# A PE-saturated attention kernel: the five score steps of a head pair in another order, issued ahead of the softmax parts, and the first pair's steps on other slots

## The chip, the cores and the metric

The kernel runs on one core of one Trainium2 chip. The metric is the device time of one execution in microseconds (us); three runs of the kernel before gave 687.08, 687.08 and 687.57, so the median is 687.08. TensorE is called PE below and its weight loads PEld, VectorE is DVE, ScalarE is ACT, GpSimd is POOL, SyncE (which issues most DMAs) is SP.

## The reference

An input x of 2048 tokens by 448 features is normalised, and two branches are added to it: attention with 16 heads of 28 features, in four segments of 512 tokens with a compressive memory, and a gated FFN of width 1792.

```python
logits = jnp.einsum("bhqd,bhkd->bhqk", qs, ks) * scale + mask   # per segment, 512 x 512
p = _softmax(logits, axis=-1)
a_dot = jnp.einsum("bhqk,bhkd->bhqd", p, vs)
a_mem = num / den                                 # recall from the memory of earlier segments
o = g * a_mem + (1.0 - g) * a_dot
...
h = _sigmoid(g) * u                               # FFN
return x + _A_ref(xn, ...) + _B_ref(xn, ...)
```

The mask keeps only a triangle of each 512 by 512 block: in this reference's orientation, with keys in four blocks of 128 rows, block kb meets 512 - 128 kb query columns: 512, 384, 256 and 128.

## The kernel before, in words

**Stages.** A front part (to about 160 us) normalises x, turns it, and computes keys, queries, values and the memory. Then the FFN runs on PE, and the attention of all segments is cut into small steps that are dropped between the FFN's matmul groups. Last comes the output projection (`project`, lines 749 to 783), which begins when the FFN's own groups are out.

**FFN.** `gated` (line 166) loops over pairs of 128 wide slices and over the four token blocks. For each slice it runs two groups of 11 matmuls of 512 columns (`pgu`, line 247), and the down projection of the block before in groups of 6 matmuls of 448 columns (`pd`, line 173).

**Attention.** A `Pair` is two heads of one segment; a `Unit` is two pairs (four heads); there are 32 pairs and 16 units. `Pair.scores` (lines 603 to 637) has five steps, n = 0 to 4. Each step runs one or two matmuls `st` (line 612) into one PSUM bank of 512 columns (tag "s", two banks), ACT copies the bank into the pair's SBUF tile `w` (line 616 or 619), POOL writes the mask into the diagonal blocks (line 627), and after some steps DVE takes maxima with a transposing reduction (`mx`, line 629 for 1024 columns, line 633 for 512). Before the change the steps are: head 0 block 512; head 0 blocks 384+128 and the reduction of head 0; head 1 block 512; head 1 blocks 384+128 and the reduction of head 1; both heads' blocks of 256 and their short reduction.

`Pair.weights` (lines 639 to 668) has five parts: the maxima are joined by small DVE and POOL operations (lines 643 to 653), DVE spreads them (`mb`, line 656), and three times DVE subtracts (line 666) and ACT takes the exponential (line 667). `Unit.finish` (lines 681 to 695) multiplies the weights of four heads with the values (`pa`, line 687, 32 matmuls in the profile), divides (lines 690 to 693) and adds the result into DRAM (`od`, line 694).

**What sets the order.** `attention` (line 700) walks for each unit over the 14 entries of `SLOT` (line 39): 0 or 1 means one score step of the unit's first or second pair, 2 means `finish` of the unit before, `None` means no step. In each slot it first gives out one part of the weights waiting in `behind`, then the second half of a `finish`, then the score step. When a pair's last score step is out, its five weight parts are appended to `behind` (line 724), and the SP queue gets the six DMAs (line 595) that load the keys and queries of the pair two further on; for the last unit these are instead the eight DMAs (line 747) of `load_sums(0)` and `load_sums(1)`, which fetch the finished attention rows for the projection. After a `finish` the unit's values are loaded (`vv`, line 679). The loop at lines 789 to 798 gives out 234 slots evenly over the FFN's and the projection's steps.

On PE and SP the program's order is kept (`MANUAL`, line 55). On ACT, DVE and POOL a planner places the instructions when the kernel is built; there the order of the program only decides which goes first when several are ready in its plan. The buffers are: `w` three, `mx` two, `mb`, `up`, `top` one, keys and queries (`qk2`) two, PSUM tag "s" two banks.

Of the kernel before, what the change touches and what calls it, by code (L numbers as in the profile page):

```python
# [16 lines left out]
P = 128  # L17
# [5 lines left out]
L = 512  # L23
# [12 lines left out]
LEAD, TAIL = 15, 53  # L36


SLOT = (0, 0, 0, None, 0, 0, None, 2, 1, 1, 1, None, 1, 1)

PARTS = 5

# [1 line left out]
HW = 1280  # L44
# [17 lines left out]
def kernel(  # L62
# [11 lines left out]
    V, A, G, T = nc.vector, nc.scalar, nc.gpsimd, nc.tensor  # L74
# [40 lines left out]
    def bank(name, tag):  # L115
        return ps.tile([P, L], F32, name=name, tag=tag, bufs=banks[tag])
# [159 lines left out]
    with tc.tile_pool(name="front", bufs=2) as sb, tc.manual_schedule(engines=FRONT):  # L276
# [227 lines left out]
        for b in range(NB):  # L504
# [24 lines left out]
            for k, c in enumerate((3, 4, 5, 6, 0, 1, 2) if last else range(7)):  # L529
# [34 lines left out]
                n = k - 1 if b == 0 else k + 1  # L564
# [18 lines left out]
    class Pair:  # L583
# [19 lines left out]
        def scores(self):  # L603

            self.w = sb.tile([P, 2 * HW], F32, name="w", bufs=3)
            w3 = self.w.rearrange("p (h n) -> p h n", h=2)
            mx = sb.tile([P, 80], F32, name="mx", bufs=2)
            for n in range(5):
                st = bank("st", "s")
                for h, kb in (((n // 2, 0),), ((n // 2, 1), (n // 2, 3)))[n % 2] if n < 4 else ((0, 2), (1, 2)):  # L610
                    at = KB[kb] % L + (256 * h if kb == 2 else 0)
                    T.matmul(st[:, at:at + L - kb * P], self.qk[:KS, 1, h, kb * P:(kb + 1) * P],  # L612
                             self.qk[:KS, 0, h, kb * P:], start=True, stop=True)
                if n < 4:
                    w = self.w[:, HW * (n // 2) + L * (n % 2):][:, :L]
                    A.activation(w, st, AF.Copy)  # L616
                else:
                    w = w3[:, :, 2 * L:]
                    A.activation(w, st.rearrange("p (h n) -> p h n", h=2), AF.Copy)

                if n % 2 == 0 and n < 4:
                    d = w[:, :P]
                    pattern = [[1, P]]
                else:
                    d = w.rearrange("p (a n) -> p a n", n=P)[:, 0:4:3, :] if n < 4 else w[:, :, :P]
                    pattern = [[0, 2], [1, P]]
                G.affine_select(d, d, pattern=pattern, base=0, channel_multiplier=-1, compare_op=ALU.is_ge, fill=MASK)  # L627
                if n in (1, 3):
                    V.tensor_reduce(mx[:, 16 * (n - 1):16 * (n + 1)],  # L629
                                    w3[:, n // 2, :2 * L].rearrange("p (b n) -> p b n", n=32),  # L630
                                    axis=mybir.AxisListType.X, op=ALU.max, apply_transpose=True)
                if n == 4:
                    V.tensor_reduce(mx[:, 64:80].rearrange("p (h b) -> p h b", h=2),
                                    w.rearrange("p h (b n) -> p h b n", n=32),
                                    axis=mybir.AxisListType.X, op=ALU.max, apply_transpose=True)
                yield
            yield from self.weights(mx)
# [60 lines left out]
    units = [Unit(u, pairs[2 * u:2 * u + 2]) for u in range(NB * NG)]  # L698

    def attention():  # L700
        for n in range(2):
            pairs[n].load()
        units[0].load_values()
        yield
        run, behind, fin = {}, [], None
        for u in range(len(units) + 1):
            for n in range(2):
                run[n] = pairs[2 * u + n].scores() if u < len(units) else iter(())
            for k, which in enumerate(SLOT):
                if u == len(units):  # L710

                    if k > 9:
                        break
                    which = ((None,) * 8 + (2, None))[k]
                if behind:
                    next(behind.pop(0))
                if fin:
                    next(fin)
                    fin = None
                if which is not None and which < 2 and u < len(units):  # L720
                    next(run[which])
                    n = 2 * u + which + 2
                    if which not in SLOT[k + 1:]:
                        behind += [run[which]] * PARTS
                        if n < len(pairs):
                            pairs[n].load()
                        else:
                            load_sums(n - len(pairs))
                if which == 2 and u > 0:
                    fin = units[u - 1].finish()  # L730
                    next(fin)
                    if u < len(units):
                        units[u].load_values()
                yield
# [3 lines left out]
    def load_sums(b):  # L738

        if b < 2:  # L740
            sums[b] = sb.tile([P, HG, L], F32, name="sums", tag="qk2", bufs=2)
        else:
            sums[b] = sums[b - 2]
        o3 = od[b].rearrange("(h c) n -> h c n", c=32)
        for m in range(8):
            a, c = m % 2, 4 * min(m, 6)
            nc.sync.dma_start(sums[b][64 * a:64 * a + 64, m // 2, :], o3[:, c:c + 4, :])  # L747
# [36 lines left out]

    N_OUT = 1 + NB * NT * 3 + 12
    steps = attention()
    n_att = len(units) * len(SLOT) + 10
    done = 0
    with tc.manual_schedule(engines=MANUAL):
        next(steps)  # L790
        k = sum(FILLS) + 6
# [46 lines left out]
```

## Time and profile before

| what | value |
|---|---|
| median of three runs | 687.08 us |
| the profiled execution | 687.17 us |
| its span, first to last instruction | 685.5 us |
| granted TensorE clock | 1.0 of full speed |
| busy: PE, DVE, PEld | 99%, 83%, 83% of the span |
| busy: ACT, POOL | 50%, 21% of the span |
| DMA | 84.37 MB, mean 123 GB/s |

The busy time of an engine is the time covered by its instructions. The end of a matmul in the profile is modelled, and matmuls overlap, so the distance from one start to the next says more than the duration of one. "Idle before" tells how long an engine stood still ahead of a group, and the name behind the arrow is what released it. A timeline row has the start in us, the length in us, the engine, the line, the operation, what it writes and reads, and how many instructions are merged into the row. Groups of one line give how often, and the minimum, median and maximum of one in ns.

### The profile page before, as it was taken

How to read it: one execution, taken by the hardware profiler on the slowest of the kernel's cores; microseconds unless marked ns; L12 is line 12 of the kernel's file. 1: busy time of each engine (PE TensorE's matmuls, PEld its weight loads, DVE VectorE, ACT ScalarE, POOL GpSimd, SP SyncE). 2: the span in 40 equal slices, each digit the busy share in tenths (PEclk: the TensorE clock that was granted, in tenths of full speed). 3: DMA queues.
4: the chain of work that ended last, by engine and by line, in shares of the span. 5: the costliest groups of instructions: out<-in, count | busy, mean ns of one | idle time of the engine just before them, and what ended most of it. 6: DMA issues, size and time to landing. Idle time of an engine off the chain costs nothing.

```text
span 685.5 us, 10454 instructions
## 1 busy us (share of the span) xinstructions
PE 680.3 (99%) x3594; PEld 566.1 (83%) x3594; DVE 567.1 (83%) x995; ACT 341.6 (50%) x563; POOL 146.6 (21%) x349
## 2 busy tenths in 40 slices
PE   8999999999999999999999999999999999999998
PEld 7898878778878787887878778787887878778897
DVE  6765695767789998988998889988998899889863
ACT  4837555343554455544556446455643465446220
POOL 3500010101223232222232222222322313212000
PEclk9999999999999999999999999999999999999999
DMA  7446556697232333243324243324342423423352
GB/s 268 178 153 232 205 205 245 244 336 182 71 95 76 95 88 86 57 126 80 90 59 107 62 126 72 99 57 117 81 99 73 97 56 83 94 77 96 92 156 107
DMA packets 45940, 84.37 MB, mean 123 GB/s; under 512 B 6336, under 2 KB 20544, under 8 KB 45376
## 3 DMA queue, kind: packets, MB, share of 16 engines
q1 hardware_dynamic: 42736, 76.26, 36.2%
q0 software_dynamic: 3008, 7.34, 5.1%
q8 instruction: 28, 0.46, 0.3%
q14 instruction: 24, 0.20, 0.1%
q10 hardware_dynamic: 144, 0.11, 0.0%
HBM read 51.05 MB, written 32.64 MB: 122 GB/s over the span
## 4 chain that ended last, share of the span: by engine, by line
PE 96%; DMA 1%; SPq 1%; DVE 1%; issue 0%; ACT 0%; DVEq 0%; ACTq 0%
PE pgu L247 41%; PE pd L173 20%; PE pp L355 10%; PE st L612 6%; PE po L771 5%; PE pa L687 5%; PE pv L335 5%; PE pmm L383 2%; PE n L401 2%; DMA acc<-in_x 1%; SPq L747 1%; PE pt L95 1%; PE pk L375 1%; DMA vv<-vd 0%; DVE stats L294 0%
## 5 line engine op out<-in xcount | busy, mean ns | idle before, releaser
L247 PE MATMUL pgu<-xs,wgu 128*128 128x512 f32 x1232 | 303.6, 393 | 0.0
L247 PEld LDWEIGHTS pgu<-xs,wgu 128*128 128x128 f32 x1232 | 228.2, 188 | 46.9 <-issue 2.4
L173 PE MATMUL pd<-wdn,hh 128*128 128x448 f32 x672 | 155.9, 367 | 0.0
L173 PEld LDWEIGHTS pd<-wdn,hh 128*128 128x128 f32 x672 | 122.4, 188 | 12.0 <-issue 0.8
L627 POOL TENSOR_SCALAR_AFFINE_SELECT w<-w 128x256 f32<-128x256 f32 (+1 forms) x160 | 79.7, 501 | 242.0 <-ACT w L616 193.1
L667 ACT ACTIVATE w<-w 128x1024 f32<-128x1024 f32 (+1 forms) x96 | 87.3, 915 | 87.3 <-DVE w L666 86.8
L666 DVE TENSOR_TENSOR w<-w,mb 128x1024 f32<-128x1024 f32 (+1 forms) x96 | 98.7, 1036 | 0.2
L616 ACT ACTIVATE w<-st 128x512 f32<-128x512 f32 x128 | 74.6, 590 | 43.5 <-PE st L612 43.2
L629 DVE TRANSPOSE_TENSOR_REDUCE mx<-w 128x32 f32<-128x1024 f32 x64 | 78.8, 1231 | 14.9 <-POOL w L627 14.9
L355 PE MATMUL pp<-xs,wqk 128*128 128x512 f32 x308 | 77.7, 401 | 0.0
L174 DVE TENSOR_TENSOR acc<-pd,acc 128x448 f32<-128x448 f32 x112 | 67.2, 600 | 1.1 <-PE pd L173 1.1
L355 PEld LDWEIGHTS pp<-xs,wqk 128*128 128x128 f32 x308 | 56.8, 188 | 13.4 <-issue 2.4
L612 PE MATMUL st<-qk 84*128 84x128 f32 (+3 forms) x256 | 62.2, 312 | 0.1
L258 ACT ACTIVATE hh<-sg 128x512 fp32r<-128x512 f32 x56 | 35.2, 628 | 52.5 <-DVE sg L256 41.9
L612 PEld LDWEIGHTS st<-qk 84*128 84x128 f32 x256 | 47.6, 189 | 7.4 <-ACT w L616 0.6
L255 ACT ACTIVATE sg<-pgu 128x512 f32<-128x512 f32 x56 | 33.1, 591 | 37.5 <-PE pgu L247 37.4
L656 DVE STREAM_TRANSPOSE mb<-top 128x1024 f32<-128x1024 f32 x32 | 39.7, 1242 | 12.5 <-POOL top L653 12.2
L362 DVE TENSOR_TENSOR qk<-pp,qk 128x512 fp32r<-128x512 f32 x28 | 19.3, 688 | 29.8 <-ACT e L360 23.7
L259 DVE SCALAR_TENSOR_TENSOR hh<-sg,hh 128x512 fp32r<-128x512 f32 x56 | 38.9, 694 | 2.8 <-ACT hh L258 2.4
L335 PE MATMUL pv<-wv,xs 128*128 128x448 f32 x176 | 39.7, 376 | 0.2
L256 DVE SCALAR_TENSOR_TENSOR sg<-sg,pgu 128x512 f32<-128x512 f32 x56 | 37.4, 667 | 1.8 <-PE pgu L247 1.6
L687 PE MATMUL pa<-w,vv 128*32 128x128 f32 (+3 forms) x512 | 37.9, 436 | 0.0
(100 smaller groups left out, 640.7 us busy)
## 6 DMA issues: line engine op xcount, KB each, us to landing
qk<-qd SPq DMA_DIRECT2D x192, 112.0 KB
qd<-qk SPq DMA_DIRECT2D x28, 512.0 KB
raw<-in_w_ffn SPq DMA_DIRECT2D x14, 512.0 KB
vd<-vst SPq DMA_DIRECT2D x4, 1024.0 KB
vv<-vd SPq DMA_DIRECT2D x16, 256.0 KB
od<-w POOLq DMA_DIRECT2D x16, 256.0 KB, 4.0
sums<-od SPq DMA_DIRECT2D x32, 128.0 KB
out<-acc SPq DMA_DIRECT2D x15, 224.0 KB
```

The source lines that it names most:

```text
L173: T.matmul(pd[:, :D], l, r, start=n == 0, stop=n == len(mms) - 1)
L174: V.tensor_add(acc[b][:, t, :], pd[:, :D], acc[b][:, t, :])
L247: T.matmul(dst, wgu[f][:, w, side * P:(side + 1) * P], xs[b][:, a, :], start=n == 0, stop=n == len(TERMS) - 1)
L335: T.matmul(pv[:, :D], xs[b][:, a, t * P:(t + 1) * P], wv[w], start=n == 0, stop=n == len(TERMS) - 1)
L355: T.matmul(pp, wqk[c][:, w, :], xs[b][:, a, :], start=n == 0, stop=n == len(TERMS) - 1)
L612: T.matmul(st[:, at:at + L - kb * P], self.qk[:KS, 1, h, kb * P:(kb + 1) * P], self.qk[:KS, 0, h, kb * P:], start=True, stop=True)
L616: A.activation(w, st, AF.Copy)
L627: G.affine_select(d, d, pattern=pattern, base=0, channel_multiplier=-1, compare_op=ALU.is_ge, fill=MASK)
L629: V.tensor_reduce(mx[:, 16 * (n - 1):16 * (n + 1)], w3[:, n // 2, :2 * L].rearrange("p (b n) -> p b n", n=32), axis=mybir.AxisListType.X, ...
L666: V.tensor_sub(w, w, m)
L667: A.activation(w, w, AF.Exp, scale=SCALE)
L687: T.matmul(pa[32 * j:32 * j + 32, kb * P:], self.vv[:, kb, 32 * j:32 * j + 32], self.pairs[j // 2].block(j % 2, kb), start=kb == 0, stop=k ...
```

## The change

Three things are changed, and nothing is computed otherwise.

The score steps of a pair come in another order: head 0 block 512; head 1 block 512; both heads' blocks of 256, with their short reduction; head 0 blocks 384+128, with head 0's reduction; head 1 blocks 384+128, with head 1's reduction.

A score step is cut in two by a `yield`: matmuls, ACT copy and POOL mask are given out first, then the weights part that is due in the slot and the second half of a `finish`, then the DVE reduction.

The first pair's steps sit on slots 1, 2, 4, 5 and 7 where they sat on 0, 1, 2, 4 and 5. The second pair's stay on 8, 9, 10, 12 and 13, and `finish` stays on 7, where the first pair's last step is now ahead of it.

```diff
-SLOT = (0, 0, 0, None, 0, 0, None, 2, 1, 1, 1, None, 1, 1)
+SLOT = ((), (0,), (0,), (), (0,), (0,), (), (0, 2), (1,), (1,), (1,), (), (1,), (1,))
...
-                for h, kb in (((n // 2, 0),), ((n // 2, 1), (n // 2, 3)))[n % 2] if n < 4 else ((0, 2), (1, 2)):
+                h = n % 2 if n < 2 else n - 3
+                for h, kb in (((h, 0),), ((0, 2), (1, 2)), ((h, 1), (h, 3)))[(0, 0, 1, 2, 2)[n]]:
...
                 G.affine_select(d, d, pattern=pattern, base=0, channel_multiplier=-1, compare_op=ALU.is_ge, fill=MASK)
-                if n in (1, 3):
-                    V.tensor_reduce(mx[:, 16 * (n - 1):16 * (n + 1)],
-                                    w3[:, n // 2, :2 * L].rearrange("p (b n) -> p b n", n=32),
+                yield
+                if n > 2:
+                    V.tensor_reduce(mx[:, 32 * h:32 * h + 32],
+                                    w3[:, h, :2 * L].rearrange("p (b n) -> p b n", n=32),
                                     axis=mybir.AxisListType.X, op=ALU.max, apply_transpose=True)
-                if n == 4:
+                if n == 2:
...
+                score = [which for which in now if which < 2]
+                part = behind.pop(0) if behind else None
+                for which in score:
+                    next(run[which])
+                if part:
+                    next(part)
                 if fin:
                     next(fin)
                     fin = None
-                if which is not None and which < 2 and u < len(units):
+                for which in score:
                     next(run[which])
                     n = 2 * u + which + 2
-                    if which not in SLOT[k + 1:]:
+                    if not any(which in later for later in SLOT[k + 1:]):
                         behind += [run[which]] * PARTS
...
-                if which == 2 and u > 0:
+                if 2 in now and u > 0:
                     fin = units[u - 1].finish()
                     next(fin)
```

More of the change, by code (lines that the diff above doesn't have):

```diff
@@ L613, in scores @@
                              self.qk[:KS, 0, h, kb * P:], start=True, stop=True)
-                if n < 4:
-                    w = self.w[:, HW * (n // 2) + L * (n % 2):][:, :L]
+                if n != 2:
+                    w = self.w[:, HW * h + L * (n // 2 > 0):][:, :L]
                     A.activation(w, st, AF.Copy)
@@ L619, in scores @@
                     A.activation(w, st.rearrange("p (h n) -> p h n", h=2), AF.Copy)
-                if n % 2 == 0 and n < 4:
+                if n < 2:
                     d = w[:, :P]
@@ L624, in scores @@
                 else:
-                    d = w.rearrange("p (a n) -> p a n", n=P)[:, 0:4:3, :] if n < 4 else w[:, :, :P]
+                    d = w.rearrange("p (a n) -> p a n", n=P)[:, 0:4:3, :] if n > 2 else w[:, :, :P]
                     pattern = [[0, 2], [1, P]]
                 G.affine_select(d, d, pattern=pattern, base=0, channel_multiplier=-1, compare_op=ALU.is_ge, fill=MASK)
-                if n in (1, 3):
-                    V.tensor_reduce(mx[:, 16 * (n - 1):16 * (n + 1)],
-                                    w3[:, n // 2, :2 * L].rearrange("p (b n) -> p b n", n=32),
+                yield
+                if n > 2:
+                    V.tensor_reduce(mx[:, 32 * h:32 * h + 32],
+                                    w3[:, h, :2 * L].rearrange("p (b n) -> p b n", n=32),
                                     axis=mybir.AxisListType.X, op=ALU.max, apply_transpose=True)
-                if n == 4:
+                if n == 2:
                     V.tensor_reduce(mx[:, 64:80].rearrange("p (h b) -> p h b", h=2),
@@ L708, in attention @@
                 run[n] = pairs[2 * u + n].scores() if u < len(units) else iter(())
-            for k, which in enumerate(SLOT):
+            for k, now in enumerate(SLOT):
                 if u == len(units):
@@ L713, in attention @@
                         break
-                    which = ((None,) * 8 + (2, None))[k]
-                if behind:
-                    next(behind.pop(0))
+                    now = (2,) if k == 8 else ()
+                score = [which for which in now if which < 2]
[4 more added lines that the diff above has]
+                    next(part)
                 if fin:
```

## The prediction

> **What bounds the kernel now.** I read the page first, for the share of each engine and for the chain that ended last.
>
> ```profile
> span 685.5 us, 10454 instructions
> PE 680.3 (99%) x3594; PEld 566.1 (83%) x3594; DVE 567.1 (83%) x995; ACT 341.6 (50%) x563; POOL 146.6 (21%) x349
> PE 96%; DMA 1%; SPq 1%; DVE 1%; issue 0%; ACT 0%; DVEq 0%; ACTq 0%
> ```
>
> PE is covered for 680.3 of 685.5 us, and 96% of the chain is PE. The ends of matmuls are modelled, so this could hide gaps. Two more views were asked: the table by stages, for where PE stands still, and PE's own timeline, for the distance from start to start.
>
> ```profile
> core 0: us, PE busy (x) PEld busy (x) DVE busy (x) ACT busy (x) POOL busy (x), PEclk, DMA share, GB/s
> 162.00:400.00 238.00, 238.00 (x1266) 196.61 (x1266) 208.75 (x340) 122.82 (x194) 60.73 (x156) 1.00 0.34 89
> 400.00:610.00 210.00, 210.00 (x1136) 172.21 (x1135) 190.18 (x305) 109.40 (x172) 54.76 (x135) 1.00 0.34 82
> 610.00:643.00 33.00, 32.94 (x196) 26.30 (x195) 30.96 (x56) 18.21 (x30) 6.21 (x15) 1.00 0.30 81
> 643.00:685.50 42.50, 39.08 (x195) 36.28 (x194) 23.84 (x48) 4.39 (x8) 0.86 (x1) 1.00 0.45 142
> ```
>
> ```profile
> 254.92 2.65 PE L247 MATMUL pgu<-xs,wgu 128*128 128x512 f32 x11
> 257.42 0.68 PE L612 MATMUL st<-qk 84*128 84x384 f32 x4
> ...
> 259.14 2.65 PE L247 MATMUL pgu<-xs,wgu 128*128 128x512 f32 x11
> 261.72 2.36 PE L687 MATMUL pa<-w,vv 128*32 128x512 f32 x32
> ```
>
> From 162 us to 610 us, which holds nearly all of the attention, PE has no idle time at all, at a full granted clock. Eleven FFN matmuls take 257.42 - 254.92 = 2.50 us from their start to the start of what follows: 0.227 us each, one after the other. The change can only take away waits of PE that stand inside this stream. These show best on PE's weight loads, which cannot run ahead of a closed wait. The list of waits, for that engine:
>
> ```profile
> PEld pa L687 <- issue: 19.1, 73, 0.4
> ...
> PEld pa L687 <- POOL w L627: 1.3, 4, 0.4
> ...
> PEld st L612 <- ACT w L616: 0.6, 2, 0.3
> ```
>
> The score steps wait for ACT to empty their bank twice in 160 steps, 0.6 us in all. The 19.1 us ahead of `pa` were released by nothing, and belong to how its 32 matmuls follow each other; the order of the score steps does not touch that. The four entries of 0.4 us named after POOL's mask are as long as the ordinary ones beside them. So the attention steps cost PE their own matmuls and at most 0.6 us, or 0.6 + 1.3 = 1.9 us if the POOL entries were real.
>
> One rule speaks against this reading. The Trainium skill, page "Perfetto Trace Analysis", section "Identifying the Most-Contended Engine", says that the busy share of matmuls is a bad measure for how full PE is, and that the busy share of the weight loads should be used. By it PE would have 17% of room here. The row of the FFN's loads answers:
>
> ```profile
> L247 PEld LDWEIGHTS pgu<-xs,wgu 128*128 128x128 f32 x1232 | 228.2, 188 | 46.9 <-issue 2.4
> ```
>
> A load takes 188 ns and its matmul's place in the gapless stream is 227 ns: 83% is what a full stream of this shape gives. What the rule would make of the time is the first rival below.
>
> **The change part by part.** *The order of the blocks.* Each pair keeps its five steps with the same eight matmuls, five copies, five masks and three reductions, so PE's own work changes by 0. What moves is the last step before the weights: it had the short reduction, and now has a long one.
>
> ```profile
> L629 DVE TRANSPOSE_TENSOR_REDUCE mx<-w x64: 1190/1236/1247, 167.8 to 627.7; 128x32 f32<-128x1024 f32 x64
> L633 DVE TRANSPOSE_TENSOR_REDUCE mx<-w x32: 656/697/712, 176.1 to 629.3; 128x16 f32<-128x512 f32 x32
> ```
>
> ```profile
> L687 PE MATMUL pa<-w,vv x512: 272/432/617, 203.2 to 642.6; 128*32 128x512 f32 x43, 128*32 128x384 f32 x43, 128*32 128x128 f32 x43, 128*32 128x256 f32 x42
> ```
>
> The chain from the last score to the exponentials grows by 1.236 - 0.697 = 0.54 us per pair. In steady state this meets cover. `pa` starts first at 203.2 us and last at 640.37 us (the row stands below), 15 units apart, so a unit takes 29.1 us and a slot 2.08 us. For the second pair, whose weights are due soonest, a reduction of 1.236 us of the first pair used to fall into slot 1, between its parts; it is now given out in slot 5, behind them, and a short one in slot 4. That gives back 1.24 us ahead of `pa` against the 0.54 us. For the first pair the parts move from slots 6 to 10 to slots 8 to 12, still 9 slots (19 us) ahead of the `pa` that reads them. I take 0, between -0.6 and +0.5 us (one `pa` that loses the 0.54).
>
> *The score step ahead of the weights part.* No instruction is added. Copies and masks come before the other pair's exponentials and joins, so that PE's bank is empty earlier:
>
> ```profile
> ACT w L667 <- DVE w L666: 86.8, 56, 6.1
> ...
> ACT w L616 <- PE st L612: 43.2, 31, 3.8
> ```
>
> ACT stands for 86.8 us in front of exponentials whose subtraction is not done, and a copy queued behind one is late with it. With the copies ahead, and with the run of score slots 12, 13, 0, 1, 2 broken (slot 0 is empty now; the longest run is 7 to 10), some of the 0.6 us should go. I take half, -0.3 us; the ends are -0.6 us and the cost of a fresh wait in each unit, 16 x 0.3 = +4.8 us, since the planner lays ACT, DVE and POOL anew and I cannot read its order here.
>
> *The first pair's slots.* Its key and query loads go out in slot 7, not 5, for use in slot 1, not 0: the distance falls from 9 slots to 8, 16.6 us.
>
> ```profile
> 258.12 2.48 SPq L595 DMA_DIRECT2D qk<-qd  x6
> ```
>
> ```profile
> od<-w POOLq DMA_DIRECT2D x16, 256.0 KB, 4.0
> ```
>
> Six issues hold SP for 2.48 us; the page has no landing time for these, and the nearest is the 4.0 us of a 256 KB transfer. Estimated at 6.5 us from those rows, they leave 10 us of cover: 0. Behind them on SP now stands `vv`, wanted a unit (29 us) later, and the FFN's weight loads: 2.5 us late at most, 0. In slot 7 `pa` follows a score matmul instead of an FFN matmul, which no row shows. Before, its entry costs 261.72 - 259.14 - 11 x 0.227 = 0.08 us. I take the same after a short matmul, with 0 and 0.2 us as ends (the second as if its loads, 8 in 0.16 us, stood fully open): -1.3 to +1.9 us over 16, both unlikely; taken 0.
>
> *The last unit.* Two things have less cover here. The end of the second pair's chain:
>
> ```profile
> 637.55 1.06 ACT L667 ACTIVATE w<-w 128x1024 f32<-128x1024 f32 x1 [3.28 <-DVE w L666]
> ...
> 640.37 2.49 PE L687 MATMUL pa<-w,vv 128*32 128x512 f32 x32
> ...
> 640.70 0.62 ACT L667 ACTIVATE w<-w 128x512 f32<-128x512 f32 x1
> ```
>
> The last exponential ends at 641.32, after `pa` has begun, and this `pa` is 0.13 us longer than the 2.36 us of the others. 0.54 us more would fall on PE nearly whole; DVE's order there may give some back. I take +0.3 us, between 0 and +0.6.
>
> Then the sums for the projection, 8 issues that slot 5 gave out and that slot 7 will:
>
> ```profile
> 609.52 6.13 SPq L747 DMA_DIRECT2D sums<-od  x8
> ...
> 613.12 2.36 PE L687 MATMUL pa<-w,vv 128*32 128x512 f32 x32
> ...
> 615.75 0.55 SPq L679 DMA_DIRECT2D vv<-vd  x1
> ...
> 616.72 0.40 PE L612 MATMUL st<-qk 84*128 84x512 f32 x1
> ...
> 619.29 0.58 ACT L616 ACTIVATE w<-st 128x512 f32<-128x512 f32 x1
> ...
> 619.46 0.96 PE L612 MATMUL st<-qk 84*128 84x384 f32 x3
> 619.76 1.66 ACT L753 ACTIVATE xs<-sums 128x512 fp32r<-128x512 f32 x3
> 619.92 0.19 PEld L612 LDWEIGHTS st<-qk 84*128 84x128 f32 x1 [0.26 <-ACT w L616]
> ```
>
> They start 613.12 - 609.52 = 3.6 us later, which the projection does not feel, since its first matmul follows the FFN. ACT may: its splits (line 753) stand among the score copies. I take 0 and keep the price for a rival.
>
> Sum: 687.17 (profiled) + 0 - 0.3 + 0 + 0 + 0.3 + 0 = 687.17. The profiled execution lies 0.09 above the median of 687.08, its 1.67 us outside the span unchanged: **687.1 us**.
>
> **The rivals.** *Faster: PE had room.* If the POOL entries are real waits and all waits of attention steps go, 1.9 us go: 685.2. By the Trainium skill's page "Perfetto Trace Analysis", section "Identifying the Most-Contended Engine", there would be still more to gain. For it speaks that no mask is late any more; against it, that these entries are no longer than those without a releaser, and that PE idles 0.00 us from 162 to 610. Chance 0.06.
>
> *Slower: the sums hold ACT.* Place: slots 8 to 10 of the last unit. If ACT's queue has a split ahead of a score copy while the sums are still in flight, the copy waits for the landing, now 3.6 us later. Then the copy of slot 8's bank moves from 619.29 to 622.9 and the third score, which came at about 619.9, waits about 3 us: 690.2. It decides from the point where ACT gets to the split before the landing; before, ACT got there just after, and PE still lost 0.26 us. Against it: the planner sees the later issue too, and would move the splits back. Chance 0.09.
>
> *Slower: fresh bank waits.* A new order on ACT puts some exponential ahead of a copy in half of the units: 8 x 0.3 = 2.4 us, 689.5. For it: only two waits are there now, so there is little to win and much to lose; against it: the copies have precedence in the new program. Chance 0.07.
>
> *The change does not do what it says.* The planner places ready copies first anyway and the three engines keep nearly their order: 687.1 too. Chance 0.04.
>
> **How the numbers follow.** The forecast has 0.74, with a range of its own of 686.4 (both waits gone, the tail at 0) to 688.2 (a `pa` late by 0.5, the tail at +0.6). The range given is 686.2 to 688.8; it leaves out the first rival, the second, and half of the third: 0.06 + 0.09 + 0.035 = 0.185. Within 0.2%, which is 1.37 us and about what a measurement of this kernel can tell from no change, lie the forecast, the last rival and a little of the third: 0.79. Faster 0.06, slower 0.15.
>
> **What would show it.** Right: PE idle 0.00 from 162 to 610 again, at most three waits of `st` for ACT, all three reductions as long as now, and the last `pa` at 640.4 to 641 us with a length of 2.4 to 3.0 us. Wrong: a list of PEld waits with more than 1 us on `st`; a `pa` entry that differs from 0.08 us; ACT idle ahead of line 753 near 620 us with a score step waiting behind it. A time under 685.7 would mean that PE had waits which this trace does not show.

## The result and the profile after

| | before | after |
|---|---|---|
| median of six runs | 687.13 us | 692.0 us |
| lowest to highest | 687.03 to 687.57 | 691.16 to 692.88 |
| the profiled execution | 687.17 us | 692.88 us |
| its span | 685.5 us | 691.2 us |

The change makes the kernel slower: ratio 1.007, 95% interval 1.0059 to 1.0081. The forecast of 687.1 and its range up to 688.8 were wrong. The six runs of after lie in two groups, three at 691.16 to 691.25 with a granted clock of 0.999 to 1.0, three at 692.76 to 692.88 with 0.997; where those 1.6 us come from is worked out below.

The page of the changed kernel, the lines that answer to the first fence of the prediction:

```profile
span 691.2 us, 10514 instructions
PE 682.5 (99%) x3594; PEld 569.6 (82%) x3594; DVE 568.0 (82%) x995; ACT 339.5 (49%) x563; POOL 140.7 (20%) x349
PE 60%; DVE 20%; issue 11%; POOL 4%; ACT 2%; DMA 1%; SPq 0%; POOLq 0%; DVEq 0%; ACTq 0%
```

The instructions of each engine are as many as before. PE is still covered for 99%, and a reader of that number alone would see nothing. The chain of work that ended last tells more: 96% of it was PE, now 60% is, and DVE has 20%. The end of the kernel now hangs on a wait that leads back to DVE. The table by stages (length, busy us of each engine, granted clock, DMA share, GB/s):

```profile
core 0: us, PE busy (x) PEld busy (x) DVE busy (x) ACT busy (x) POOL busy (x), PEclk, DMA share, GB/s
162.00:400.00 238.00, 236.74 (x1260) 196.39 (x1259) 208.03 (x333) 120.20 (x192) 57.87 (x149) 1.00 0.34 88
400.00:610.00 210.00, 207.80 (x1112) 170.87 (x1111) 185.84 (x305) 106.55 (x170) 50.64 (x138) 0.99 0.36 84
610.00:643.00 33.00, 33.00 (x178) 27.46 (x177) 30.52 (x50) 18.55 (x30) 7.45 (x19) 1.00 0.32 81
```

Where PE had no idle time between 162 and 610 us, it now has 1.26 and 2.20 us. The list of waits of PE's weight loads (us in total, times, longest) names them:

```profile
PEld pa L689 <- issue: 14.4, 57, 0.3
PEld st L613 <- ACT w L620: 3.7, 2, 2.0
...
PEld pa L689 <- ACT w L669: 1.0, 3, 0.4
...
PEld st L613 <- ACT w L617: 0.9, 1, 0.9
```

One kind has grown and one is new. Score steps wait three times for the ACT copy that empties their bank (lines 617 and 620), 4.6 us in all where it was 0.6. And `pa` waits for exponentials (line 669), which it did nowhere in the list of before.

**The account of the 5.7 us.** For each matmul the trace has a start, so the distance to the next start can be compared with the median distance after a matmul of that kind. Added up over the distances that begin or end at a score matmul, those above their median exceed it by 4.72 us, against 1.20 before: **+3.5**. The 16 runs of 32 `pa` matmuls, each from its first start to the next matmul's start, take 38.22 us against 36.78: **+1.4**. Before, 15 of them took 2.29 us and the last 2.42; now four take 2.75, 2.37, 2.75 and 2.80. The matmuls of the FFN are spaced wider behind one of the waits, **+1.6**, as the clock falls there. The remaining **-0.8** is what is left over, many small differences in the spacing of matmuls, with no single one to name. 3.5 + 1.4 + 1.6 - 0.8 = 5.7, the difference of the spans.

**One score wait, read from the timeline.** Around 600 us, the second pair of the last but one unit:

```profile
594.93 0.40 PE L613 MATMUL st<-qk 84*128 84x256 f32 x2
...
597.63 1.21 DVE L668 TENSOR_TENSOR w<-w,mb 128x1024 f32<-128x1024 f32 x1
...
598.93 1.06 ACT L669 ACTIVATE w<-w 128x1024 f32<-128x1024 f32 x1 [5.71 <-DVE w L668]
...
599.89 0.61 ACT L258 ACTIVATE hh<-sg 128x512 fp32r<-128x512 f32 x1
...
600.41 0.57 ACT L620 ACTIVATE w<-st 128x512 f32<-128x512 f32 x1
...
601.04 0.50 PE L613 MATMUL st<-qk 84*128 84x384 f32 x2 [1.78 <-ACT w L620]
601.38 2.34 PE L173 MATMUL pd<-wdn,hh 128*128 128x448 f32 x6
```

Step 2, the blocks of 256, filled its bank by 595.33 us. Its copy (line 620) needs nothing else and takes 0.57 us. But in ACT's queue it stands behind an exponential, and that one stands 5.71 us for the subtraction on DVE (line 668). The copy starts at 600.41, 5.1 us late, and step 4, which needs the same bank (there are two), holds PE for 1.78 us. The other two have the same form, a ready copy behind ACT work that came late from DVE: 1.26 us of PE's idle time at 321.35, the copy behind two exponentials, and 0.4 us near 418, where the copy stands not behind an exponential but behind an instruction of the FFN (`hh`, line 258) that had stood 2.36 us for DVE.

**What follows the wait.** The granted clock in the stretches just behind it:

```profile
601.00:603.50 2.50, 2.46 (x8) 2.23 (x9) 2.03 (x5) 2.36 (x4) 0.85 (x2) 0.62 0.24 80
603.50:607.00 3.50, 3.50 (x14) 2.81 (x13) 3.24 (x6) 0.66 (x2) 0.41 (x1) 0.78 0.61 139
607.00:610.00 3.00, 3.00 (x15) 2.61 (x14) 1.68 (x5) 1.72 (x3) 1.48 (x5) 1.00 0.00 0
...
601.60:605.00 3.40, 3.40 (x10) 2.85 (x10) 2.93 (x5) 2.43 (x5) 0.82 (x2) 0.50 0.57 150
```

0.62 and 0.78 are means. Cut at other times, as in the last row, the granted clock is 0.50 from 601.6 to 605.0 us, and it is 1.00 on both sides. 3.4 x 0.5 = 1.7 us of clock are lost. That is the distance of the two groups of runs, 692.8 - 691.2 = 1.6.

**One `pa` wait.** `pa` multiplies the weights of both pairs. In the timeline of one unit of after:

```profile
496.17 1.06 ACT L669 ACTIVATE w<-w 128x1024 f32<-128x1024 f32 x1 [3.88 <-DVE w L668]
...
498.08 1.56 ACT L669 ACTIVATE w<-w 128x1024 f32<-128x1024 f32 x2
...
498.32 2.87 PE L689 MATMUL pa<-w,vv 128*32 128x512 f32 x32
```

The first exponential of the second pair stood 3.88 us for DVE, so the last two run while `pa` is already at work, and end at 499.64. Of the 32 matmuls the last ones wait inside the group, and it takes 2.80 us from start to next start. The end of the last exponential lay about 1.4 us ahead of the start of `pa` before (median of 16), and lies about 0.15 us behind it now. Not every late end costs: with the end up to 0.57 us behind its start a group still takes 2.29 us, and in after the six whose end lies 0.85 to 1.33 us behind take 2.32 to 2.80.

### The profile page after: what moved, and what is told of

It is laid out like the page before. It is cut to its first block, busy times and chain, and to the rows that moved or that the text cites. A ratio compares the mean times of both kernels' runs of the same rounds, so it can differ in the third digit from the quotient of the medians.

```text
span 691.2 us, 10514 instructions
## 1 busy us (share of the span) xinstructions
PE 682.5 (99%) x3594; PEld 569.6 (82%) x3594; DVE 568.0 (82%) x995; ACT 339.5 (49%) x563; POOL 140.7 (20%) x349
## 4 chain that ended last, share of the span: by engine, by line
PE 60%; DVE 20%; issue 11%; POOL 4%; ACT 2%; DMA 1%; SPq 0%; POOLq 0%; DVEq 0%; ACTq 0%
PE pgu L247 21%; PE pd L173 10%; PE pp L355 10%; PE po L777 5%; DVE mx L631 5%; PE pv L335 5%; DVE w L668 3%; PE st L613 3%; DVE acc L174 2%; PE pa L689 2%; POOL w L628 2%; DVE hh L259 2%; PE pmm L383 2%; PE n L401 1%; DVE sg L256 1%
## 5 line engine op out<-in xcount | busy, mean ns | idle before, releaser
L628 POOL TENSOR_SCALAR_AFFINE_SELECT w<-w 128x256 f32<-128x256 f32 (+1 forms) x160 | 68.9, 433 | 246.1 <-ACT w L617 180.2
L689 PE MATMUL pa<-w,vv 128*32 128x128 f32 (+3 forms) x512 | 39.3, 436 | 0.0
```

The costliest lines, as they stand in the source:

```text
L689: T.matmul(pa[32 * j:32 * j + 32, kb * P:], self.vv[:, kb, 32 * j:32 * j + 32], self.pairs[j // 2].block(j % 2, kb), start=kb == 0, stop=k ...
```

## Which part does it

The theory after these readings: (1) ACT's queue keeps its order, so a late DVE subtraction holds a copy that is ready, and PE with it; (2) the new order or places make the subtractions late. The rivals: the early hand-out itself puts ACT in a bad order; the new entry of `pa` costs; or the planner's order is a matter of chance and any edit would cost as much. The three parts were taken apart in six kernels. In this table B is the order of the blocks, A the early hand-out with the score step cut in two, P the places of the first pair; "score" is the sum by which score steps exceed their medians, "pa" the sum of the 16 groups, both of the profiled execution.

| kernel | parts | us | ratio, 95% interval | score | pa |
|---|---|---|---|---|---|
| before | none | 687.13 | 1 | 1.20 | 36.78 |
| e5 | A | 687.21 | 1.0 (0.9991 to 1.0009) | 1.44 | 36.80 |
| e6 | B | 690.10 | 1.0041 (1.0027 to 1.0055) | 2.90 | 37.96 |
| e4 | P | 689.35 | 1.0031 (1.0019 to 1.0043) | 1.50 | 38.29 |
| e1 | B, A | 689.08 | 1.0028 (1.0017 to 1.0039) | 1.96 | 37.91 |
| e2 | A, P | 689.60 | 1.0035 (1.0021 to 1.0048) | 1.22 | 38.55 |
| e3 | B, P | 692.18 | 1.0076 (1.0059 to 1.0093) | 5.50 | 37.38 |
| after | B, A, P | 692.0 | 1.007 (1.0059 to 1.0081) | 4.72 | 38.22 |

The first four (e1 to e4) were expected to lie at 686.8 to 687.8 or at 690 to 692, by one theory or another. e1, e2 and e4 lie between the two and e3 just above the second, so no part alone carries the whole loss, and the theory that put it all on the places was wrong.

**The first pair on its old places (e1).**

```diff
-SLOT = ((), (0,), (0,), (), (0,), (0,), (), (0, 2), (1,), (1,), (1,), (), (1,), (1,))
+SLOT = ((0,), (0,), (0,), (), (0,), (0,), (), (2,), (1,), (1,), (1,), (), (1,), (1,))
```

> The changed kernel with the first pair's steps back on slots 0, 1, 2, 4, 5; new block order and the early hand-out stay. Theory (the places do it: the copy of the first pair's slot 4 step stands on ACT behind the second pair's exponentials, which wait for late DVE subtractions, and its bank is asked for again in slot 7 instead of slot 8): 686.8 to 687.8, no wait of a score step for ACT above 0.5 us. Rival A (the long reduction at the end of a pair makes DVE and with it the exponentials late): 690 to 692. Rival B (the early hand-out does it): 690 to 692.

689.08 us: 2.9 us of the 4.9 come back. The three long score waits are gone, and no score step's wait is new. At 451 us it is an FFN group behind a score step that loses 0.72 us, which the column "score" counts with the rest. And two `pa` take 3.01 and 2.84 us. So the new places are needed for the long score waits, and not for the late `pa`.

**The old order of the blocks (e2).**

```diff
-                h = n % 2 if n < 2 else n - 3
-                for h, kb in (((h, 0),), ((0, 2), (1, 2)), ((h, 1), (h, 3)))[(0, 0, 1, 2, 2)[n]]:
+                for h, kb in (((n // 2, 0),), ((n // 2, 1), (n // 2, 3)))[n % 2] if n < 4 else ((0, 2), (1, 2)):
```

> The changed kernel with the old order of the score blocks; the new places and the early hand-out stay. Theory (places): 690 to 692, waits of 1 to 2 us of the slot 7 step for a copy. Rival A (long reduction last): 686.8 to 687.8. Rival B (early hand-out): 690 to 692.

689.60 us. Score waits are as few as before, and `pa` is the worst of the six: 2.88, 3.37 and 2.49 us. Either part alone delays `pa`; in these six kernels score waits over 1 us are only where both are there.

**No early hand-out (e3).**

```diff
-                yield
...
-                for which in score:
-                    next(run[which])
-                if part:
-                    next(part)
+                if part:
+                    next(part)
```

> The changed kernel with each score step whole and given out behind the weights part of its slot, as before; new block order and new places stay. Theory (places): 690 to 692. Rival A (long reduction last): 690 to 692. Rival B (early hand-out): 686.8 to 687.8.

692.18 us, as slow as after, with 1.10 us at 427 and the wait of 1.94 us at 600.6 again. The early hand-out neither makes the loss nor prevents it. The granted clock was 0.997 and 0.998 in two of its four runs too, 692.81 and 693.03 us against 691.37 and 691.55.

**The places alone (e4)**, before with the new `SLOT`.

```diff
-SLOT = (0, 0, 0, None, 0, 0, None, 2, 1, 1, 1, None, 1, 1)
+SLOT = ((), (0,), (0,), (), (0,), (0,), (), (0, 2), (1,), (1,), (1,), (), (1,), (1,))
```

> The kernel before with the new places alone. Theory (places): 690 to 692. Rivals A and B: 686.8 to 687.8. If it lies near 687 and the first kernel of this set does too, the places need one of the other two parts to do harm.

689.35 us, +2.2. `pa` is 1.5 us longer in sum, in two groups of 2.77 and 3.45 us. PE's and ACT's timelines of the second one:

```profile
408.04 1.70 PE L687 MATMUL pa<-w,vv 128*32 128x512 f32 x12
410.06 1.49 PE L687 MATMUL pa<-w,vv 128*32 128x384 f32 x20 [0.33 <-ACT w L667]
```

```profile
404.64 1.06 ACT L667 ACTIVATE w<-w 128x1024 f32<-128x1024 f32 x1 [4.24 <-DVE w L666]
...
408.03 1.06 ACT L667 ACTIVATE w<-w 128x1024 f32<-128x1024 f32 x1
409.38 0.63 ACT L667 ACTIVATE w<-w 128x512 f32<-128x512 f32 x1 [0.29 <-DVE w L666]
```

The first exponential stood 4.24 us for DVE, the last one ends at 410.01, and the thirteenth `pa` matmul starts at 410.06. In before the last exponential of this unit began at 406.33, and its `pa` at 407.48.

**The hand-out alone (e5)**, before with the step cut in two and given out first.

```diff
                 G.affine_select(d, d, pattern=pattern, base=0, channel_multiplier=-1, compare_op=ALU.is_ge, fill=MASK)
+                yield
...
+                for which in score:
+                    next(run[which])
+                if part:
+                    next(part)
```

> The kernel before with the early hand-out of a score step alone (old block order, old places). New theory, formed after the first four runs (two separate harms: the new places squeeze the second pair's weights, so that the matmuls of pa wait for the last exponentials, about 1.5 us in all; the new block order puts the copy of the 256+256 step behind late exponentials, so that a later score step waits for its bank; the early hand-out does neither): 686.8 to 687.6, pa at 36.8 us in all 16. Rival (any new plan of ACT and DVE loses some 2 us, whatever the edit): 688.5 to 690.

687.21 us, ratio 1.0 with 0.0009 to each side. Score waits and `pa` are nearly those of before. This speaks against the rival that any edit to the order costs, but weakly: in its trace only some 13 of ACT's 563 instructions and 9 of DVE's 995 stand at another place in their engine's order than in before, and PE's order is the same.

**The blocks alone (e6)**, before with the two lines that e2 takes out of after.

> The kernel before with the new block order alone (old places, no early hand-out). Theory: as with the hand-out, 688.6 to 689.4, with waits of pa in the fourth and the last unit (about 1 us) and one or two score waits (0.3 to 0.8 us). Rival (any new plan loses 2 us): 688.5 to 690, with the waits at other places than in the first of these runs.

690.10 us, +2.9, above both of the ranges given: two `pa` of 3.08 and 2.80 us, score waits of 0.18 to 0.26 us, and a loss of 0.83 us at 451. The last is no score step's wait. PE's list of waits has no score step, but this:

```profile
PE pgu L247 <- ACT sg L255: 0.7, 1, 0.7
```

The FFN's group waits for ACT to empty its own bank (line 255), and in ACT's queue that instruction stands behind three exponentials, the first of which stood 4.17 us for DVE. So the late ACT work reaches PE by a third way, which the column "score" holds as well.

With the places' 2.2 the 2.9 make 5.1, and both together (e3) cost 5.0, or 4.3 in its two executions at a full clock. The sums are close, but not place by place: in e3 `pa` is longer by 0.6 us, where e4 and e6 have 1.5 and 1.2, and the score steps make up for it with 4.3. That the two parts add up is therefore not shown.

## What makes them late

**The weights' parts two slots later in before (e7).** The places put the first pair's parts into slots 8 to 12, with one free slot ahead of the second pair's (0 to 4 of the next unit), where before it was 6 to 10 and three. This kernel moves the parts and leaves the score steps in place.

```diff
-                        behind += [run[which]] * PARTS
+                        behind += [repeat(None)] * (2 - 2 * which) + [run[which]] * PARTS
```

> The kernel before with all score steps and loads on their old places, but the first pair's five weight parts two slots later (slots 8 to 12, as with the new places). Theory (it is the first pair's subtractions and exponentials two slots later that delay the second pair's, and so pa): 688.5 to 689.5, waits inside pa of 1 to 2 us in all, hardly any score waits. Rival (the places harm by the score steps themselves or by the later loads): 686.8 to 687.6, pa at 36.8 us in all 16.

690.51 us, ratio 1.0047 (1.0032 to 1.0062). The harm is there, but it is 1 us more than I gave at most, and not where I expected it: I looked for a late `pa` and hardly any score waits. `pa` grew by 0.57 us, in one group, and the score steps by 2.7 (0.40 at 281, 0.45 at 368, 1.46 at 390). The timeline of the last:

```profile
388.13 1.06 ACT L668 ACTIVATE w<-w 128x1024 f32<-128x1024 f32 x1 [5.16 <-DVE w L667]
...
389.09 0.58 ACT L617 ACTIVATE w<-st 128x512 f32<-128x512 f32 x1
...
389.72 0.51 PE L613 MATMUL st<-qk 84*128 84x512 f32 x1 [1.29 <-ACT w L617]
```

The same picture, in the old order of blocks and on the old places: an exponential that stands for DVE, a copy behind it, a score step behind the copy. So a move of the parts alone is enough for the mechanism, and whether the delay shows at `pa` or at a score step is not fixed by it.

**Less work on DVE (e8 and e9).** Both leave out the short reduction and its join: the maxima do not see the blocks of 256, which takes 32 reductions of about 0.70 us and 32 joins from DVE.

```diff
-                if n == 2:
-                    V.tensor_reduce(mx[:, 64:80].rearrange("p (h b) -> p h b", h=2),
...
-            V.tensor_max(m0[:, :, 8:16], m0[:, :, 8:16], mx[:, 64:80].rearrange("p (h n) -> p h n", h=2))
```

> The changed kernel without the short reduction of each pair and the joining of its result (the maxima then leave out the blocks of 256), 0.87 us less on DVE per pair and 28 us in all. Theory (DVE is late, exponentials wait for its subtractions and hold up what stands behind them on ACT): score waits and pa waits both fall to under half, 687.0 to 689.0, and the clock stays at 1.0. Rival (the order on ACT alone decides, not how late DVE is): 690.5 to 692.5, with score waits of 1 to 2 us left.

In the changed kernel: 685.35 us, ratio to before 0.9973 (0.9962 to 0.9983), where I had expected 687.0 to 689.0. All that was lost is gone, and 1.9 us more. Table by stages and waits of PE's loads:

```profile
162.00:400.00 238.00, 238.00 (x1268) 197.59 (x1267) 199.42 (x309) 121.18 (x193) 61.73 (x155) 1.00 0.35 91
400.00:610.00 210.00, 210.00 (x1138) 173.59 (x1138) 180.53 (x277) 111.00 (x175) 57.03 (x135) 1.00 0.35 81
```

```profile
PEld pa L684 <- issue: 16.0, 65, 0.3
...
PEld st L613 <- issue: 0.2, 1, 0.2
```

PE has no idle time there, no score step waits for ACT, and all 16 `pa` take 2.29 us. This is the one kernel that beats both, and it leaves work out. The control, the same left out of before:

> The kernel before without the short reduction and the joining of its result (the maxima then leave out the blocks of 256). It is the control for the last run of the set before, which had the changed kernel at 685.35. Theory (with DVE relieved the changed order is worth some 1.7 us, in the short gaps between PE's matmuls and in score waits; the harm comes from a late DVE alone): 686.6 to 687.1, so that the changed order is ahead by 1.2 to 1.8 us. Rival (the 1.9 us come from the work left out, whatever the order): 685.0 to 685.8.

688.61 us, ratio 1.0019 (1.001 to 1.0029), slower with less work. Both numbers that I had given were missed. All `pa` are in time (36.66 us), but there is a new score wait of 1.42 us:

```profile
209.66 0.60 ACT L255 ACTIVATE sg<-pgu 128x512 f32<-128x512 f32 x1 [3.84 <-PE pgu L247]
...
210.93 1.06 ACT L662 ACTIVATE w<-w 128x1024 f32<-128x1024 f32 x1 [0.68 <-DVE w L661]
...
211.90 0.58 ACT L616 ACTIVATE w<-st 128x512 f32<-128x512 f32 x1
...
212.53 0.50 PE L612 MATMUL st<-qk 84*128 84x512 f32 x1 [1.25 <-ACT w L616]
```

The copy is once more behind an exponential, and this time DVE was only 0.68 us late. Of the theory this leaves: late subtractions make such waits likely, but the planner's order of ACT decides whether one arises, and it lays that order anew for each program. Less work on DVE is no warranty.

**The step of 256 earlier (e10)**, on slot 3 instead of 4, for the first pair of the changed kernel.

```diff
-SLOT = ((), (0,), (0,), (), (0,), (0,), (), (0, 2), (1,), (1,), (1,), (), (1,), (1,))
+SLOT = ((), (0,), (0,), (0,), (), (0,), (), (0, 2), (1,), (1,), (1,), (), (1,), (1,))
```

> The changed kernel with the first pair's third step (256+256) on slot 3 where it had slot 4, all else as changed. Theory (the copy of that step stands on ACT behind two exponentials of the second pair, and its bank is asked for again in slot 7): one exponential less ahead of it and one slot more of room, so the two waits of 1.4 and 1.9 us at 321 and 601 us go, and with them the low clock; the waits of pa stay: 688.0 to 689.8. Rival (three score steps in a row on slots 1, 2, 3 bring a wait of their own): 690 to 692.

689.92 us, ratio 1.0038 (1.0023 to 1.0053), a little above what I had given. The wait at 321, a first pair's, is gone; that at 600, a second pair's, stays with 1.22 us, and new ones came at 371 (0.43) and 482 (0.72); one `pa` takes 3.73 us. The granted clock was 1.0 in all four runs.

**The FFN's split on POOL (e11, e12).** To take work from DVE without leaving anything out, the low half of each split weight goes to POOL, in the changed kernel and in before.

```diff
-        V.tensor_sub(lo, src, hi.bitcast(F32))
+        G.tensor_sub(lo, src, hi.bitcast(F32))
```

> The changed kernel with the low halves of the FFN's weights (line 86) subtracted on POOL where DVE did it: 27.2 us less on DVE, nothing left out. Theory (late DVE is the cause): score waits and pa waits fall to under a third, 685.2 to 687.5. Rival (POOL's masks come late in its place, or DVE's lateness is not the cause): 688.5 to 692.

> The kernel before with the same subtractions on POOL. Theory: it had hardly any waits to lose: 686.5 to 687.2, behind the changed kernel with the same edit. Rival: 687.2 to 689, if POOL's masks come late.

702.76 us (1.0225, 1.0209 to 1.024) and 706.19 us (1.0276, 1.0261 to 1.0292): both theories' numbers were far off, and the pair tells nothing about DVE, since it breaks something else. The groups and the waits of e12:

```profile
L86 POOL TENSOR_TENSOR wgu<-raw,wgu 128x1024 fp32r<-128x1024 f32 x14 | 35.3, 2522 | 35.0 <-ACT wgu L85 34.7
```

```profile
ACT w L667 <- DVE w L666: 113.3, 54, 6.7
...
POOL wgu L86 <- ACT wgu L85: 34.7, 8, 12.9
...
PEld st L612 <- ACT w L616: 12.5, 8, 4.6
```

POOL stands up to 12.9 us for a weight's high half. ACT stands 113.3 us for DVE, against 86.8 in before, and the score steps wait up to 4.6 us behind it. The longest of these waits, from the timeline:

```profile
206.92 2.40 POOL L86 TENSOR_TENSOR wgu<-raw,wgu 128x1024 fp32r<-128x1024 f32 x1
...
209.38 0.55 POOL L652 COPY top<-top 32x32 f32<-32x32 f32 x1
...
213.81 1.06 ACT L667 ACTIVATE w<-w 128x1024 f32<-128x1024 f32 x1 [6.67 <-DVE w L666]
...
215.41 0.79 PE L612 MATMUL st<-qk 84*128 84x512 f32 x1 [4.25 <-ACT w L616]
```

A small copy that joins the maxima (line 652) stands behind the split on POOL, the spreading and the subtraction on DVE come after it, and from there it is the same mechanism, here with POOL at its root.

## One copy moved

The direct test: the changed kernel with one edge more, which puts the 256 copy of pair 29 (the one read above) ahead of the exponential behind which it stood. PE's, SP's and POOL's orders stay; on ACT one instruction moves, on DVE one short reduction moves up by two places.

```diff
                     copy = A.activation(w, st.rearrange("p (h n) -> p h n", h=2), AF.Copy)
+                    if self.n in AHEAD:
+                        held.append(copy)
...
+                if held:
+                    tc.add_manual_dep(exps[-1].ins, held.pop().ins.name, mybir.DependencyInfo(
```

> The changed kernel with one edge for the planner: the copy of the 256+256 step of pair 29 has to stand ahead of the next exponential. PE, SP and POOL keep their order; on ACT this one copy moves ahead of one exponential and one cast, on DVE one short reduction moves up two places. Theory (the order on ACT at single places does the harm: a copy behind an exponential whose subtraction is late): the wait of 1.9 us at 601 us goes, with it the low clock after it, and nothing else changes: 688.8 to 689.6, granted clock 0.999 or more in every run. Rival (late work on DVE is what PE waits for, and the wait only moves to the next place): 690.5 to 692.5.

690.51 us, ratio 1.005 (1.0035 to 1.0065): 1.5 us less than after, and 0.7 less than its executions at a full clock. I had expected 688.8 to 689.6; the rival's 690.5 to 692.5 holds it. The timeline:

```profile
595.82 0.60 ACT L626 ACTIVATE w<-st 128x512 f32<-128x512 f32 x1 [2.15 <-PE st L619]
...
599.32 0.68 PE L619 MATMUL st<-qk 84*128 84x384 f32 x4
599.38 1.06 ACT L680 ACTIVATE w<-w 128x1024 f32<-128x1024 f32 x1 [2.96 <-DVE w L679]
```

The copy runs at 595.82 instead of 600.41, and the score step at 599.32 waits for nothing. The clock stayed at 0.999 to 1.0 in all four runs, and in the stretches where it had been 0.62 and 0.78 it is 1.00. At the last `pa` the kernel is 3.1 us ahead of after (643.05 against 646.19). But then:

```profile
643.05 1.70 PE L703 MATMUL pa<-w,vv 128*32 128x512 f32 x12
...
645.25 1.05 PE L703 MATMUL pa<-w,vv 128*32 128x384 f32 x14 [0.51 <-ACT w L680]
```

`pa` comes earlier, the exponentials do not; it takes 3.62 us where it took 2.32, and 1.3 us are given back. PE's wait had hidden that DVE was late.

**Two copies moved (e14)**, the same for pair 10, whose copy held the step at 321.

```diff
-BEHIND = {}
+BEHIND = {10: 1}
```

> As the run beside it, and the copy of the 256+256 step of pair 10 has to stand ahead of the second exponential before it too (three small moves on ACT there, none on DVE). Theory: the wait of 1.4 us at 321 us goes as well; what stays are the waits inside pa (1.4 us in all) and one of 0.6 us: 687.4 to 688.3. Rival: 689 to 692.

689.81 us, ratio 1.0037 (1.0022 to 1.0051). I had expected 687.4 to 688.3, and the rival's 689 to 692 holds the time. The wait at 321 falls from 1.43 to 0.16 us and that at 418 from 0.59 to 0.29, so ACT's order was what held them. But the `pa` behind them now take 2.46 and 3.02 us, where after had 2.29 and 2.37. Score steps are at 1.15 us, better than before; `pa` is at 40.36 us, 3.6 worse. ACT's order is the way the delay took, and DVE's late work is what lies behind it.

## Where the prediction failed, step by step

- **What bounds the kernel:** right. PE was full from 162 to 610 us, and an edit could only lose there, but for the 1.9 us that e8 found.
- **The steps that failed** are the two terms taken at 0, the order of the blocks and the first pair's slots, and with them the wait of the score steps, which the prediction weighed only under the early hand-out, at -0.3 us. Each alone costs more than 2 us (2.9 in e6, 2.2 in e4), by late `pa` and by ACT work held behind DVE; all three together cost 4.9, with +3.5 us at the score steps.
- **The score step ahead of the weights part, "I take half, -0.3 us":** its reason, that copies "come before the other pair's exponentials and joins", is about the order in which steps are given out; e5 shows that this alone changes nothing (less than 0.1 us, with 0.6 to each side). In the whole change the score steps cost +3.5 us. The upper end of +4.8 us, the cost of a fresh wait in each unit, did hold it, but as 16 waits of 0.3; there were three of 0.6 to 1.9. A wait's length need not be that of the two that the trace of before had: it can come near the time that ACT stands for DVE, and that row (longest 6.1 us) was quoted beside the sentence.
- **The order of the blocks, "I take 0, between -0.6 and +0.5":** wrong. e6 alone costs 2.9 us. The 0.54 us by which the chain grows was right as a sum per pair; that the earlier long reduction gives back 1.24 us ahead of `pa` was argued from slots and did not come: `pa` is 1.2 us longer in e6, and an FFN group that the prediction did not look at loses 0.8.
- **The first pair's slots, taken 0:** wrong, though not by the terms that it names. The loads were in time, as worked out, and the entry of `pa` behind a score matmul is 152 ns for a matmul of 60 ns, 92 ns more; before it was 318 for 227, 91 more. So the 0.08 us that I took was right. What the step left out was the five weights parts: it counted how far they lie from the `pa` that reads them (9 slots) and not how near they come to the second pair's, which share DVE with them. The new slots cost 2.2 us in e4, and the parts alone, two slots later, 3.3 in e7.
- **The last unit, +0.3 us:** its `pa` took 2.32 us against 2.42, so 0.1 less; DVE had more time there because PE came later. e13 shows the other case, 3.62.
- **The rivals:** the fresh bank waits were the right kind, at 2.4 us and a chance of 0.07; the price was 1.1 short for the waits alone, and `pa` and clock were not in it. The sums behind the projection hold nothing: no score step waits for ACT near 620 us. That PE had room came true only in e8, 685.35 us for 685.2, with less work on DVE and no wait of the attention steps, and not by the 17% that the rule on loads gives.
- **The signs named for a wrong forecast:** "more than 1 us on `st`" is what the list shows, 4.6 us.

**What stays open.** Why the old program has only short waits and each of these edits but e5 has long ones is not settled by a rule: the planner's order is remade each time, and e9 shows a wait of 1.42 us where DVE has less to do. Shown is how the waits that were read come about, that moving the copy removes two of them, and that the blocks and the places cost 2.9 and 2.2 us, each in one build. Whether these prices belong to the parts, or to the order that the planner happened to lay for each of them, is not separated. That it is the nearness of the two pairs' parts which makes the places costly is argued from the slots. e7 speaks for it in size, but it has the loss mostly at score steps, where e4 has it mostly at `pa`. A version that keeps all of the computation and beats before was not found.

## What to carry to other kernels

An engine that works through its queue in order passes on the lateness of any other, as ACT did here with DVE's: ahead of moving work between engines' queues, look for the longest time that a queue stands in front of an instruction that is not ready (here ACT for DVE, 6.1 us), since a ready instruction behind it can be as late as that, and take that as the price of a bad place, not the mean of the waits now seen. If work of two streams shares an engine that is 87% to 91% busy, as DVE is here from 162 to 610 us, count the distance between the streams and not only from each to its reader; this is the part that is argued here and not shown. And when one wait is removed, look for the same delay at the next consumer: here half of what came back at the score steps was lost at `pa`.

## What the hardware showed besides

The clock of PE fell after a wait of 1.78 us in the middle of a full stream: to 0.50 of full speed from 601.6 to 605.0 us, which made a wait of 1.8 us cost 3.5. By the mean granted clock of 0.997 it did so in three of six executions of after. It did not after the wait of 1.26 us at 321 us, where the granted clock is 1.00 in the profile, nor in the profiled execution of e3, where PE waited the same 1.78 us before 600.58 and the granted clock stayed at 1.00. In e12 it was 0.50 from 371.4 to 374.7 us, behind a wait of 2.52 us. The Trainium skill, page "TensorE: Matmul & The Clock Gate", section "What's actually happening", says that the clock halves after an idle window of about 3.4 us, and that the window runs freely, so that the point differs from run to run. That it comes in some executions and not in others agrees with the second, and the 0.50 with the halving; the length does not fit here, as PE's idle stretch was about half as long.

POOL takes 2522 ns in e12 for the subtraction of two tiles of 128x1024 that takes 1227 ns on DVE in before.
